# Rebuilding the start-up of a two-layer transformer kernel: first norm transposed on TensorE, bf16 input kept, a second home for one chunk's queries and keys, projections of the third chunk pulled forward

## The chip, the cores and the metric

The kernel runs on one core of one Trainium2 chip. The metric is device time in microseconds, the median of several executions. The kernel before takes 970.37 us (968.58 to 971.06). Ratios are the mean time of one kernel's runs over that of the other's runs of the same rounds, so they are not quite the ratio of the medians quoted beside them. The kernel before was run again in every set of rounds, and its own median lay between 969.2 and 972.0 us; so a difference between medians of different sets is good to some 3 us only, and the ratios decide.

"Chunk" means 512 of the 2048 rows; two layers of four chunks make eight. Attention is done in groups of four heads, eight groups per chunk, six exponentials per group, in three pairs. "Last exponential" means the start of the last of a chunk's 24 pairs, read from the single instructions (the timelines below merge neighbours into one line); the last one ends 1.1 us later. "Block start" means the first matmul of the first feed-forward block: up to there lies the ramp, which is what the change rebuilds.

## The reference

```python
def _A_ref(x, wqkv, wo):            # 32 heads of 18, causal window of 256
    q, k, v = ...                   # x @ wqkv
    scores = einsum("bhqd,bhkd->bhqk", q, k) * (Dh ** -0.5)
    scores = where(mask, scores, -1e9)          # 0 <= i - j < 256
    o = einsum("bhqk,bhkd->bhqd", softmax(scores), v)
    return o.transpose(...).reshape(B, S, D) @ wo

def _B_ref(x, w1, b1, w2, b2):      # D = 576, F = 4608
    h = gelu(_layernorm(x) @ w1 + b1)
    return h @ w2 + b2

x = x + _A_ref(_layernorm(x), ...)  # S = 2048
x = x + _B_ref(_layernorm(x), ...)
x = x + _A_ref(_layernorm(x), ...)  # the same weights again
x = x + _B_ref(_layernorm(x), ...)
```

## The kernel before

Every operation is recorded as a task with an assumed cost. A list scheduler then fixes the order of each engine's instructions; on the chip each engine works through its list in order. Where the scheduler sees a gap on TensorE in the first 140 us, it inserts warm-up matmuls on zeros.

```python
FILL = (6, 5, 4)      # PSUM banks of projections and output matmuls
SC = (0, 2, 4)        # pairs of banks of scores
# schedule(): of all released tasks take the one that can start first
for e in ENGS:
    for t in released[e]:
        st = max(free[e], t.ready)
        ...                                       # and its PSUM banks are free
        key = (round(st, 3), t.prio, t.idx)
        if best is None or key < best[0]:
            best = (key, t, st, got)
_, t, st, got = best
if t.eng == "pe" and st < self.warm_until and st - free["pe"] > 0.4:
    self.keep_warm(free["pe"], st, bank_free, extra)
free[t.eng] = st + t.cost
```

The priority counts only between tasks that can start at the same moment.

```python
def ln_norm_T(t, i, dst, dname, prio, src=None, ...):   # normalise, then transpose
    add("dve", lambda e: e.tensor_scalar(xn[:, sl, 0:D], s[:, t, :], ...), cost=0.6)
    add("sp", lambda e: e.dma_start_transpose(dst[...], xn[:, sl, :]), lat=2.5)

def two_out(lhs, rhs, reads, prio, after=()):  # one projection or output: 2 x 5 matmuls
    bs = [Bank(FILL), Bank(FILL)]
    ...
# tail(k), per tile: output matmuls, residual, norm, and
            add("pool", lambda e, t=t: e.tensor_tensor(x_res[:, t, :], x_res[:, t, :], b2bc[:, :], ALU.add),
                reads=["b2"], writes=X(t), cost=1.4, prio=prio + 3)
# start: the two bias loads first on GpSimd's queue; chunk 0's x, then float32 x of chunk 1
    x_load(CH[1][1], CH[1][2], [f"xa{n0 - 1}"], -6)
```

The softmax here doesn't subtract the row's maximum and nothing guards it: scores larger than these inputs give would overflow.

Of the kernel before, what the change touches and what calls it, by code (L numbers as in the profile page):

```python
# [336 lines left out]
def build_kernel(nc, A_x, A_wqkv, A_wo, B_x, B_w1, B_b1, B_w2, B_b2, out):  # L337
# [56 lines left out]
    fence = sb("fence", [P, 1], FP32)  # L394
# [28 lines left out]

    def dma(q, out_, in_, reads=(), writes=(), cls="w", ring=8, **kw):
        n = 2 if cls != "xr" else 4
        for s in out_.shape:
            n *= s
        add(q, lambda e: e.dma_start(out_, in_), reads=reads, writes=writes, dma=cls, ring=ring, lat=1.3, move=n / 270e3, **kw)

    n0 = CH[0][2]  # L430
    dma("sp", x_in[:, 0:n0, :], x_dram[0:n0 * P, :].rearrange("(t p) d -> p t d", p=P), writes=[f"xin{t}" for t in range(n0)], cls="x",
        ring=4, cost=0.6, prio=-10)
# [7 lines left out]
    def x_load(a, cnt, reads, prio):  # L440

        dma("pool", x_res[:, a:a + cnt, :], x_dram[a * P:(a + cnt) * P, :].rearrange("(t p) d -> p t d", p=P), reads=reads,
            writes=[r for t in range(a, a + cnt) for r in X(t)], cls="xr", ring=8, cost=1.2, prio=prio)
# [3 lines left out]
    add("pool", lambda e: e.memset(nhalf[:, :], -0.5), writes=["nhalf"], cost=0.1, prio=-10)  # L447
    add("pool", lambda e: e.memset(xn[:, :, D:KD * 128], 0.0), writes=[f"xn{i}" for i in range(NXN)], cost=0.4, prio=-10)
    add("pool", lambda e: e.memset(vA[:, :, :, DH:VW], 1.0), writes=[f"v{s}h{h}" for s in range(VS) for h in range(2)], cost=1.6, prio=-8)
    for i in range(NQN):  # L450
# [5 lines left out]
    dma("pool", b2bc[:, :], bass.AP(tensor=B_b2.tensor, offset=B_b2.offset, ap=[[0, P], [1, D]]), writes=["b2"], cls="b", ring=2,  # L456
        cost=1.0, prio=-7)

    def load_b1(e):
        src = bass.AP(tensor=B_b1.tensor, offset=B_b1.offset, ap=[[1, P], [P, NF], [1, 1]])  # L460
        with nc.allow_non_contiguous_dma(reason="bias column layout (init only)"):
            return e.dma_start(b1col[:, :], src)
    add("pool", load_b1, writes=["b1"], dma="b", ring=2, cost=2.0, lat=10.0, prio=-7)

# [12 lines left out]
    def ln_stats(t, prio, src=None, srcres=None):  # L477
        for i in range(2):
            res = [f"x{t}h{i}"] if srcres is None else [srcres]
            s = x_res if src is None else src  # L480
            add("dve", lambda e, i=i, s=s: e.bn_stats(st_all[:, t, i, :], s[:, t, i * HB:(i + 1) * HB]),  # L481
                reads=res, writes=[f"st{t}_{i}"], cost=0.43, prio=prio)
        add("dve", lambda e: e.bn_aggr(mv_all[:, t, :], st_all[:, t, :, :]), reads=[f"st{t}_0", f"st{t}_1"], writes=[f"mv{t}"],  # L483
            cost=0.21, prio=prio)
# [14 lines left out]
    def ln_norm_T(t, i, dst, dname, prio, src=None, srcres=None, dup=False):  # L499
        s = x_res if src is None else src  # L500
        res = X(t) if srcres is None else [srcres]
        sl = xn_ctr[0] % NXN
        xn_ctr[0] += 1
        add("dve", lambda e: e.tensor_scalar(xn[:, sl, 0:D], s[:, t, :], mv_all[:, t, 0:1], rstd[:, t:t + 1],  # L504
                                              op0=ALU.subtract, op1=ALU.mult),
            reads=res + [f"mv{t}", f"rstd{t}"], writes=[f"xn{sl}"], cost=0.6, prio=prio)
        rd = [f"xn{sl}"]
        if dup:
            add("dve", lambda e: e.tensor_scalar(xn[:, sl, D:KD * 128], s[:, t, 512:D], mv_all[:, t, 0:1], rstd[:, t:t + 1],  # L509
                                                  op0=ALU.subtract, op1=ALU.mult),  # L510
                reads=res + [f"mv{t}", f"rstd{t}"], writes=[f"xd{sl}"], cost=0.12, prio=prio)
            rd.append(f"xd{sl}")
        add("sp", lambda e: e.dma_start_transpose(dst[:, :, i * 128:(i + 1) * 128], xn[:, sl, :]),
            reads=rd, writes=[f"{dname}{i}"], dma="t", ring=8, cost=1.3, lat=2.5, move=0.6, prio=prio)
# [26 lines left out]
    def two_out(lhs, rhs, reads, prio, after=()):  # L541

        bs = [Bank(FILL), Bank(FILL)]
# [13 lines left out]
    def qkv(k, i, prio):  # L557
        l, t0, nt = CH[k]
        A = l * NT + t0 + i
        for n, w in enumerate("qkv"):  # L560
            dest = [f"v{A % VS}h{o}" for o in range(2)] if w == "v" else [f"qn{qn_ctr[0] % NQN}h{o}" for o in range(2)]
            bs = two_out(lambda c: xnTa[:, c, i * 128:(i + 1) * 128], lambda c, s, n=n: wqkv[:, c, n * D + s:n * D + s + HB],
                         [f"w{w}A", f"w{w}B", f"w{w}C", f"xa{i}"], prio + 0.01 * n, after=dest)
# [6 lines left out]
            else:  # L570
# [7 lines left out]
                if w == "q":  # L578
                    dst, dn = qT[:, :, i * 128:(i + 1) * 128], f"q{i}"
                else:  # L580
                    dst, dn = kT[:, :, A % KS, :], f"k{A % KS}"
# [16 lines left out]
    def scores(k, g, parts, prio):  # L598
        l, t0, nt = CH[k]
        T0 = l * NT + t0  # L600
        sl = pcount[0] % PS
# [3 lines left out]
        def fn(e):  # L605
            ins = None
            for (so, qo, nq, col) in parts:
                for j in range(4):
                    ins = e.matmul(two(bs[j // 2])[:, j % 2, col:col + nq * 128], kT[32 * j:32 * j + 32, g, (T0 + so) % KS, :],  # L609
                                   qT[32 * j:32 * j + 32, g, qo * 128:(qo + nq) * 128], start=True, stop=True, tile_position=(32 * j, 0))  # L610
            return ins
        rd = [f"q{qo + i}" for (so, qo, nq, col) in parts for i in range(nq)] + [f"k{(T0 + p[0]) % KS}" for p in parts]
# [31 lines left out]
    def pv(k, g, parts, sl, first, last, prio):  # L644
# [18 lines left out]
        if last:  # L663
# [3 lines left out]
                prio=prio)  # L667
# [4 lines left out]
                prio=prio)  # L672
# [23 lines left out]
    def tail(k, prio):  # L696
# [5 lines left out]
        for i in range(nt):  # L702
# [3 lines left out]
            for o in range(2):  # L706
# [4 lines left out]
            add("pool", lambda e, t=t: e.tensor_tensor(x_res[:, t, :], x_res[:, t, :], b2bc[:, :], ALU.add),  # L711
                reads=["b2"], writes=X(t), cost=1.4, prio=prio + 3)


    def G_part(k, hf, prio):
# [6 lines left out]
        while f < f1:  # L722
# [18 lines left out]
            for ff, bk in zip(fs, bks):  # L741
                fl = ff - hf * NFH

                def fn(e, ff=ff, sl=sl, bk=bk):
# [8 lines left out]
                    reads=[bk, "b1"], writes=[f"h{fl}"], cost=0.2 + n * 0.00087, lat=0.2, fifo="act", prio=prio)  # L753
            if fs[-1] % 4 == 3:
                w1_load(prio - 2)
        table("exp", prio)
# [43 lines left out]
    for t in range(n0):  # L800
        ln_stats(t, -6, x_in, f"xin{t}")
    for i in range(n0):
        ln_rstd([i], False, -20)
        ln_norm_T(i, i, xnTa, "xa", -6, x_in, f"xin{i}")
    x_load(CH[1][1], CH[1][2], [f"xa{n0 - 1}"], -6)
    w_load(2, ["xa0"])
    for i in range(n0):
        qkv(0, i, -5)
    x_load(0, n0, [f"k{n0 - 1}"], -4)
    def stats0(k):  # L810
# [4 lines left out]
    stats0(1)  # L815
    ln1(1, -0.9)
    add("pool", lambda e: e.memset(fence[:, :], 0.0), reads=[f"xin{t}" for t in range(n0)], writes=[f"h{f}" for f in range(NFH)],
        cost=0.1, prio=-4)
# [5 lines left out]
    for k in range(NK + 1):  # L824
        b = 4 * k
        last = k == NK
        if not last:
            if 0 < k < NK - 1:
                ln1(k + 1, b + 1)
            E(k, range(0, 4), b - 0.5)  # L830
            if k == 0:
                wo_load()
                kk = later[0]
                x_load(CH[kk][1], CH[kk][2], ["aq1"], 0)
                stats0(kk)
# [6 lines left out]
        if k == 1:  # L842
            w2_load(0, 1, True)
            for n, kk in enumerate(later[1:]):
                x_load(CH[kk][1], CH[kk][2], [f"h{6 + 6 * n}"], b + 2)
                stats0(kk)
        if not last:
            E(k, range(4, 8), b + 1.5)
            if k == 0:
                w1_load(-1, ["aq5"])  # L850
                w1_load(-1, ["aq7"])
        if k >= 1:
            mm2(k - 1, 0, b + 2)
            w2_load(1, b + 3)
        if not last:
            if k + 1 < NK:
                for i in range(CH[k + 1][2]):
                    qkv(k + 1, i, b + 2.2 + 0.2 * i)
            tail(k, b + 1.9)
# [56 lines left out]
```

## Time and profile before

| reading | view | value |
|---|---|---|
| TensorE busy | busy table | 933.4 of 967.4 us |
| warm-up matmuls | groups by line | 284, 38.7 us |
| first projection | TensorE timeline | 14.29 us |
| first score exponential | ScalarE timeline | 32.5 us |
| last exponential of chunk 0 | ScalarE's instructions | 78.8 us |
| block start | TensorE timeline | 121.42 us |

The page's busy table, and its rows of TensorE busy and granted TensorE clock in tenths over 40 equal slices of 24.2 us:

```profile
PE 933.4 (96%) x9596; PEld 582.3 (60%) x9596; DVE 324.6 (34%) x803; ACT 588.0 (61%) x705; POOL 370.5 (38%) x507
PE   8898898999999999999999999999999999999998
PEclk9999898999999999999999999999999999999999
```

TensorE is full from the eighth slice on; the loss is in the first seven. But "busy" includes warm-up matmuls. Groups by line (busy us, mean ns of one, idle before):

```profile
L470 PE MATMUL ps<-warm 128*128 128x256 bf16 x284 | 38.7, 289 | 1.1 <-DVE warm L465 1.1
```

The timeline of TensorE (start, length, engine, line, operation, count, and in brackets the idle time before with what ended it):

```profile
1.12 11.92 PE L470 MATMUL ps<-warm 128*128 128x256 bf16 x90 [1.12 <-DVE warm L465]
14.29 6.29 PE L548 MATMUL ps<-wqkv,xnTa 128*128 128x288 bf16 x50 [1.26 <-DMA xnTa<-xn]
...
32.15 0.34 PE L609 MATMUL ps<-qT,kT 32*128 32x384 bf16 x4
...
121.42 0.61 PE L736 MATMUL ps<-xnTm,w_sb 64*128 64x512 bf16 x4
```

Nothing but filler runs for 14.29 us: tile 0's statistics start when the input is there, at 5.95; the reciprocal root stands behind the issue of a bias load on GpSimd (7.58 to 9.48); and the norm, done at 10.57, goes through a DMA transpose, the last 3.7 us. ScalarE's timeline in chunk 0's attention shows two speeds:

```profile
54.23 1.94 ACT L618 ACTIVATE pT<-ps 128x1024 bf16<-128x1024 f32 x2 [0.96 <-PE ps L609]
57.31 0.60 ACT L618 ACTIVATE pT<-ps 128x512 bf16<-128x512 f32 x1 [1.14 <-PE ps L609]
...
59.30 1.51 ACT L618 ACTIVATE pT<-ps 128x768 bf16<-128x768 f32 x2 [0.91 <-PE ps L609]
...
67.62 4.39 ACT L618 ACTIVATE pT<-ps 128x1024 bf16<-128x1024 f32 x6 [0.84 <-PE ps L609]
72.31 4.39 ACT L618 ACTIVATE pT<-ps 128x1024 bf16<-128x1024 f32 x6 [0.31 <-PE ps L609]
77.00 2.92 ACT L618 ACTIVATE pT<-ps 128x1024 bf16<-128x1024 f32 x4 [0.30 <-PE ps L609]
```

From 67.62 to 72.31 a group takes 4.69 us, nearly all ScalarE's own 4.39. From 44 to 59 us, with chunk 1's projections running, the exponentials wait about 1 us each time for scores, and a group takes about 7.5 us. Later, VectorE's norms and GpSimd's bias adds stand in each other's way. VectorE's timeline, then GpSimd's:

```profile
98.84 1.34 DVE L504 TENSOR_SCALAR xn<-x_res,mv_all,rstd 128x576 bf16<-128x576 f32 x1 [0.55 <-POOL rstd L494]
...
101.49 1.65 DVE L504 TENSOR_SCALAR xn<-x_res,mv_all,rstd 128x576 bf16<-128x576 f32 x1
...
103.65 0.56 DVE L504 TENSOR_SCALAR xn<-x_res,mv_all,rstd 128x576 bf16<-128x576 f32 x1
```

```profile
101.42 1.40 POOL L711 TENSOR_TENSOR x_res<-x_res,b2bc 128x576 f32<-128x576 f32 x1
```

The norm at 103.65 us takes 0.56 us; beside GpSimd's add it takes 1.65 (the one of 1.34 us lies beside a mask of GpSimd, 98.77 to 99.87). The Trainium skill, "SBUF — State Buffer", section "SBUF: two separate sides", says that these two engines contend, for some kinds of instruction, for one shared port pair, locked for a whole instruction, so that the other blocks. The times fit: the two long norms ended 0.32 and 0.31 us after GpSimd's instruction.

### The profile page before, as it was taken

The numbers are of one execution on the slowest core, as the hardware profiler recorded it, in microseconds if no ns is written. First come the engines' busy times: TensorE is split into PE (matmuls) and PEld (weight loads), VectorE is DVE, ScalarE is ACT, GpSimd is POOL, SyncE is SP. The second block draws the span as 40 slices with busy tenths as digits, with TensorE's granted clock in tenths as the row PEclk, the third lists the DMA queues.
The fourth block names the chain that finished last, engine by engine and source line by source line (L and its number), as shares of the span: only waits on it lengthen the run. The fifth ranks groups of instructions, "written<-read, shape, count | busy, mean of one in ns | idle before, by whom it ended". The sixth has DMA issues, their size and how long they took to land.

```text
span 967.4 us, 23096 instructions
## 1 busy us (share of the span) xinstructions
PE 933.4 (96%) x9596; PEld 582.3 (60%) x9596; DVE 324.6 (34%) x803; ACT 588.0 (61%) x705; POOL 370.5 (38%) x507
## 2 busy tenths in 40 slices
PE   8898898999999999999999999999999999999998
PEld 6665545656575655746476564756556464656556
DVE  5653711533037331454038240362214410133001
ACT  0466666478763768557761777737675487862531
POOL 4465815345153443335153251534333351532000
PEclk9999898999999999999999999999999999999999
DMA  9957380993359442694619633495527916084540
GB/s 194 178 122 137 78 250 9 209 194 112 98 127 177 102 138 72 133 204 94 182 58 197 149 112 98 78 224 114 155 68 150 201 45 196 21 219 124 179 135 25
DMA packets 242264, 129.59 MB, mean 134 GB/s; under 512 B 161393, under 2 KB 239985, under 8 KB 242161
## 3 DMA queue, kind: packets, MB, share of 16 engines
q1 hardware_dynamic: 232848, 120.43, 53.0%
q0 software_dynamic: 6880, 5.03, 2.7%
q10 hardware_dynamic: 2432, 2.65, 0.9%
q8 instruction: 76, 1.25, 0.5%
q14 instruction: 28, 0.22, 0.1%
HBM read 90.69 MB, written 2.36 MB: 96 GB/s over the span
## 4 chain that ended last, share of the span: by engine, by line
PE 82%; DMA 6%; POOL 4%; DVE 3%; issue 2%; ACT 2%; SPq 0%; POOLq 0%; DVEq 0%
PE ps L772 29%; PE ps L748 24%; PE ps L548 12%; PE ps L656 7%; PE ps L609 6%; PE ps L736 4%; POOL pT L639 2%; ACT pT L618 2%; DMA attT<-attq 2%; DVE x_res L690 1%; DMA xnTa<-xn 1%; DVE st_all L481 1%; DMA x_res<-in_A_x_dram 1%; DMA kT<-qn 1%; DMA xnTm<-xn 1%
## 5 line engine op out<-in xcount | busy, mean ns | idle before, releaser
L618 ACT ACTIVATE pT<-ps 128x1024 bf16<-128x1024 f32 (+2 forms) x384 | 347.8, 970 | 140.8 <-PE ps L609 139.1
L639 POOL TENSOR_SCALAR_AFFINE_SELECT pT<-pT 128x512 bf16<-128x512 bf16 (+1 forms) x368 | 279.2, 782 | 355.2 <-ACT pT L618 339.0
L751 ACT ACTIVATE hT<-ps,b1col 128x512 bf16<-128x512 f32 x288 | 197.9, 688 | 215.7 <-PE ps L748 215.1
L772 PE MATMUL ps<-w_sb,hT 128*128 128x288 bf16 x2304 | 316.8, 288 | 5.6 <-DVE x_res L690 3.6
L748 PE MATMUL ps<-xnTm,w_sb 128*128 128x512 bf16 x1152 | 266.3, 380 | 0.0
L772 PEld LDWEIGHTS ps<-w_sb,hT 128*128 128x128 bf16 x2304 | 211.3, 98 | 81.6 <-issue 19.6
L748 PEld LDWEIGHTS ps<-xnTm,w_sb 128*128 128x128 bf16 x1152 | 105.8, 98 | 141.1 <-issue 28.6
L690 DVE TENSOR_TENSOR x_res<-ps,x_res 128x288 f32<-128x288 f32 x160 | 71.0, 449 | 352.5 <-PE ps L772 323.3
L548 PE MATMUL ps<-wqkv,xnTa 128*128 128x288 bf16 x960 | 129.9, 287 | 5.1 <-DMA xnTa<-xn 2.1
L656 PEld LDWEIGHTS ps<-vA,pT 128*128 128x128 bf16 x2880 | 95.4, 96 | 26.9 <-issue 8.0
L548 PEld LDWEIGHTS ps<-wqkv,xnTa 128*128 128x128 bf16 x960 | 89.1, 98 | 34.4 <-issue 4.7
L656 PE MATMUL ps<-vA,pT 128*128 128x20 bf16 x2880 | 100.4, 172 | 7.0 <-POOL pT L639 3.8
L609 PE MATMUL ps<-qT,kT 32*128 32x384 bf16 (+2 forms) x1408 | 74.5, 279 | 6.6 <-ACT pT L618 4.3
L575 DVE CAST qn<-ps 128x288 bf16<-128x288 f32 x128 | 58.2, 456 | 39.3 <-PE ps L548 38.6
L504 DVE TENSOR_SCALAR xn<-x_res,mv_all,rstd 128x576 bf16<-128x576 f32 x60 | 44.8, 754 | 43.2 <-DMA xnTm<-xn 26.2
L481 DVE BATCH_NORM_STATS2 st_all<-x_res 128x6 f32<-128x288 f32 x120 | 51.0, 445 | 18.9 <-DMA x_res<-in_A_x_dram 17.5
L711 POOL TENSOR_TENSOR x_res<-x_res,b2bc 128x576 f32<-128x576 f32 x32 | 45.7, 1429 | 26.9 <-DVE xn L509 23.6
L492 POOL TENSOR_SCALAR vtmp<-mv_all 128x1 f32<-128x1 f32 (+1 forms) x43 | 8.5, 198 | 103.2 <-DVE mv_all L483 100.5
L609 PEld LDWEIGHTS ps<-qT,kT 32*128 32x128 bf16 x1408 | 22.4, 92 | 42.5 <-issue 25.2
L548 PE MATMUL ps<-wo_sb,attT 128*128 128x288 bf16 x320 | 43.2, 286 | 4.3 <-DMA attT<-attq 3.1
L693 DVE TENSOR_TENSOR xn<-ps,x_res 128x288 bf16<-128x288 f32 x32 | 14.7, 458 | 93.3 <-PE ps L772 93.3
L736 PE MATMUL ps<-xnTm,w_sb 64*128 64x512 bf16 x288 | 45.0, 382 | 0.9 <-ACT pT L618 0.9
(30 smaller groups left out, 290.0 us busy)
## 6 DMA issues: line engine op xcount, KB each, us to landing
w_sb<-in_B_w_dram SPq DMA_DIRECT2D x144, 288.0 KB, 5.0
w_sb<-in_B_w_dram SPq DMA_DIRECT2D x72, 512.0 KB, 4.2
w_sb<-in_B_w_dram SPq DMA_DIRECT2D x144, 32.0 KB, 3.8
x_res<-in_A_x_dram POOLq DMA_DIRECT2D x4, 1152.0 KB, 7.0
out_dram<-xn SPq DMA_DIRECT2D x16, 144.0 KB, 2.0
wqkv<-in_A_wqkv_dram ACTq DMA_DIRECT2D x3, 576.0 KB, 6.0
hT<-in_A_x_dram SPq DMA_DIRECT2D x1, 576.0 KB, 5.1
wo_sb<-in_A_wo_dram ACTq DMA_DIRECT2D x1, 576.0 KB, 3.9
```

The source lines that it names most:

```text
L481: add("dve", lambda e, i=i, s=s: e.bn_stats(st_all[:, t, i, :], s[:, t, i * HB:(i + 1) * HB]), reads=res, writes=[f"st{t}_{i}"], cost=0.43 ...
L548: ins = e.matmul(bank(bs[o])[:, 0:HB], lhs(c), rhs(c, o * HB), start=(c == 0), stop=(c == KD - 1))
L575: add("dve", lambda e, o=o, b=bs[o], qv=qv: e.tensor_copy(qv[:, o * 16:(o + 1) * 16, 0:DH], bank(b)[:, 0:HB].rearrange("p (h d) -> p h d", ...
L609: ins = e.matmul(two(bs[j // 2])[:, j % 2, col:col + nq * 128], kT[32 * j:32 * j + 32, g, (T0 + so) % KS, :], qT[32 * j:32 * j + 32, g, qo ...
L618: add("act", lambda e, h2=h2: e.activation(pT[:, sl, 2 * h2:2 * h2 + 2, lo:hi], two(bs[h2])[:, :, lo:hi], ACT.Exp, scale=SCALE), reads=[bs ...
L639: add("pool", lambda e, ap=ap, pat=pat, sgn=sgn, kind=kind: e.affine_select(ap, ap, pattern=pat, compare_op=(ALU.is_ge if kind == "d" else ...
L656: ins = e.matmul(bank(B_O)[:, o:o + VW], pT[:, sl, j, col + qi * 128:col + (qi + 1) * 128], vA[:, (T0 + so) % VS, 4 * g + j, :], start=(fi ...
L690: add("dve", lambda e: e.tensor_tensor(x_res[:, t, sl], bank(b)[:, 0:HB], x_res[:, t, sl], ALU.add), reads=[b], writes=[f"x{t}h{hh}"], cos ...
L736: ins = e.matmul(bank(bk)[:, 0:n], w1_sb[64 * b:64 * b + 64, sl, col:col + 128], xnTm[64 * b:64 * b + 64, k % 2, 4, 0:n], start=True, stop ...
L748: ins = e.matmul(bank(bk)[:, 0:n], w1_sb[:, sl, col:col + 128], xnTm[:, k % 2, c, 0:n], start=False, stop=(c == 3))
L751: add("act", lambda e, ff=ff, fl=fl, bk=bk: e.activation(hT[:, fl, 0:n], bank(bk)[:, 0:n], ACT.Gelu_apprx_tanh, bias=b1col[:, ff:ff + 1]), ...
L772: ins = e.matmul(bank(b)[:, 0:HB], hT[:, fl, i * 128:(i + 1) * 128], w2_sb[:, fl, hh * HB:(hh + 1) * HB], start=(fl == 0), stop=(fl == NFH ...
```

## The change

The intent is to fill the some 50 us of the ramp (38.7 of filler, 15.0 idle) in which TensorE has nothing useful to do: an earlier first projection, an earlier first score, and chunk 2's projections (120 matmuls, 60 of which the kernel before does after the block start) as useful filler in the ramp. The core of the diff:

```diff
+    qx = x_res[:, 12:16, :]...bitcast(BF16)...      # second home of chunk 1's queries
+    kx = x_res[:, 8:12, :]...bitcast(BF16)...       # and keys, in rows not loaded yet
+    def q_of(k):
+        return (qx, "qx") if k == 1 else (qT, "q")
...
+    for a, cnt in ((0, 1), (1, 1), (2, 2)):         # tile 0 arrives first
+        xin_load(a, cnt)
-    dma("pool", b2bc[:, :], ...)                     # bias loads, first on the queue
-    add("pool", load_b1, ..., prio=-7)
+    add("pool", load_b1, reads=["xa3"], ..., prio=-1)
...
+        if pe:                                       # in ln_norm_T, first four tiles
+            b = Bank(FILL)
+                for c in range(KD):
+                    ins = e.transpose(bank(b)..., xn[:, sl, c * 128:(c + 1) * 128], ident[:, :])
+            add("act", lambda e: e.copy(dst[...], bank(b)...), cost=0.75)
+            return
...
+    QK0 = {("q", 0): -5.0, ("k", 0): -4.9, ...}      # queries and keys before values
-             [...], prio + 0.01 * n, after=dest)
+             [...], prio + 0.01 * n, after=dest, fill=(6,) if k == 1 else FILL)
...
-            add("pool", ... b2bc ..., reads=["b2"])           # tail(): moved
+            if hf == 0 and fs[0] // 4 < nt:                    # into the feed-forward part
+                add("pool", ... b2bc ..., reads=["b2", f"h{fs[0]}"])
...
-    x_load(CH[1][1], CH[1][2], [f"xa{n0 - 1}"], -6)
+    xin_load(4, 4, ["xa0"], -6)                      # bf16 input of chunks 1 and 2 kept in
+    xin_load(8, 4, ["k3"], -4)                       # the space of the feed-forward result
+    ln1_in(1, -0.9)                                  # norms straight from the bf16 input
...
+            if k == 0:
+                ln1_in(2, 1)                         # chunk 2's norms in the ramp
```

## The prediction

> **What bounds the kernel.** TensorE is busy 933 of 967 us (busy table); the chain of waits is 82% TensorE. From 160 us on it is busy 98% or more of nearly every 20 us window at granted clock 1.00, so every later stage is useful TensorE work that the change leaves alone. What can be saved is in the ramp. There TensorE's "busy" is partly filler: the group of warm-up matmuls has 284 instructions at about 0.113 us apart (8 took 0.9 us), 32 us. With some 15 us idle that is about 48 us without useful work before the first feed-forward block starts at 121.4 us (timeline).
>
> Where those 48 us are (timeline, chain): 14.3 us until the first projection (input 5.1 us, reciprocal root delayed by the 1.9 us bias load on GpSimd, DMA transpose 3.6 us); first scores only at 32.2 us, because the last key transposes took 7.9 us beside the 1.15 MB float32 load of x; chunk 0's attention, with chunk 1's projections in the same PSUM banks, takes 32.5 to 82 us, though alone it runs at 4.7 us a group (ScalarE 4.39), 37.5 us for eight; from 62 us TensorE has nothing but filler, since chunk 2 cannot be projected; then chunk 1's queries wait for transposes (83 to 88), and 98 to 104 us stand still while VectorE's float32 norm (1.3 to 1.65 us against 0.58 alone) and GpSimd's bias adds (1.4 us) alternate. The Trainium skill, "SBUF - State Buffer", says those two engines share a port pair held for a whole instruction; the trace agrees.
>
> **What the change does.** 20 TensorE transposes (the skill's "TensorE: Matmul & The Clock Gate", Part 4, gives 275 to 390 ns in isolation; no trace here shows one; I estimate 0.6 us for five pipelined) and four ScalarE copies (about 0.8 us) replace four DMA transposes; tile 0 arrives first; the bias loads come later. First projection: about 8.8 us. Scores start at 22 to 26 us: 16 evictions at 0.61 us plus statistics on VectorE, and eight transpose issues at 1.4 to 1.9 us. Chunk 0's attention then runs near ScalarE's rate, end 62 to 66 us; half of chunk 1 (6.1 us a group, four groups) ends near 91. TensorE's useful work up to there is 400 projection matmuls (49.4 us at 0.1235), 40 output ones (4.9), attention 27, in all 82 us from 8.8: again 91. Both limits are tight, so I add 5 us for their friction: first feed-forward block at 96 us (91 to 103) instead of 121.4, with all of chunk 2 projected instead of half (60 matmuls, 7.4 us). Expected gain 33 us.
>
> Given back: the second half of chunk 1's attention loses those 60 matmuls of filler and becomes ScalarE-bound at its end (3 to 5 us idle, maybe a cold clock; before, 140 to 160 us also ran at 0.83). Chunks 2 and 3's x loads come later, which should stay hidden. Net about 30 us: **940 us, 8 in 10 between 927 and 954**; faster by over 2%: 0.82, within 2%: 0.16, slower: 0.02.
>
> **Right if:** warm-up matmuls fall to 71; first projection at 8 to 10 us; first score exponential at 22 to 26 us; exponentials of chunk 0 with under 15% idle; no 5 us hole near 100 us; first feed-forward block at 91 to 103 us; windows after 200 us unchanged.
>
> **Wrong if:** the one PSUM bank left to chunk 1's projections (matmuls, then eviction, serial) or the now more crowded transposes (x, queries, keys, and the b1 load's small packets at 12 us) slow chunk 0's attention; chunk 1 waits for its queries; or the saved time returns as idle TensorE in chunk 1's second half because projections there are gone.

## The result and the profile after

The changed kernel takes **957.20 us** (955.22 to 957.70), ratio 0.9863 with a 95% interval of 0.9847 to 0.9879. It is 13.2 us faster, which is within 2%, and slower than the whole predicted range of 927 to 954. All outputs are right.

| | before | predicted | after |
|---|---|---|---|
| warm-up matmuls | 284 | 71 | 71 |
| first projection, us | 14.29 | 8.8 | 9.23 |
| first exponential | 32.5 | 22–26 | 25.8 |
| end of chunk 0's attention (end of its last exponential) | 79.9 | 62–66 | 77.2 |
| block start | 121.42 | 96 (91–103) | 110.27 |
| block start to end | 846.0 | +3 | 843.6 |
| projections before the block | 300 | all of chunk 2's | 360 |

The page after, busy table, slices and warm-up group:

```profile
PE 914.3 (96%) x9403; PEld 564.0 (59%) x9403; DVE 313.7 (33%) x804; ACT 590.7 (62%) x709; POOL 369.1 (39%) x507
PE   8799899999999999999999999999999999999998
PEclk9799999999999999999999999999999999999999
```

```profile
L490 PE MATMUL ps<-warm 128*128 128x256 bf16 x71 | 12.3, 335 | 1.1 <-DVE warm L485 1.1
```

Filler fell from 38.7 to 12.3 us. But the second slice has a clock of 0.7: the ramp now has a cold spot there, where the kernel before had none (its own, of 0.8, is in the fifth slice). TensorE's timeline after:

```profile
7.92 0.44 PE L539 MATMUL ps<-ident,xn 128*128 128x128 bf16 x5
...
9.23 1.39 PE L580 MATMUL ps<-wqkv,xnTa 128*128 128x288 bf16 x10 [0.22 <-ACT xnTa L542]
...
25.40 0.34 PE L646 MATMUL ps<-qT,kT 32*128 32x384 bf16 x4 [2.78 <-DMA qT<-qn]
...
33.86 0.79 PE L580 MATMUL ps<-wqkv,xnTa 128*128 128x288 bf16 x5 [0.23 <-DVE qn L610]
...
36.93 0.29 PE L646 MATMUL ps<-qT,kT 32*128 32x256 bf16 x4 [1.13 <-ACT pT L655]
...
38.33 0.34 PE L646 MATMUL ps<-qT,kT 32*128 32x384 bf16 x4 [0.72 <-ACT pT L655]
...
41.13 1.38 PE L580 MATMUL ps<-wqkv,xnTa 128*128 128x288 bf16 x5
...
110.27 0.61 PE L771 MATMUL ps<-xnTm,w_sb 64*128 64x512 bf16 x4
```

ScalarE's timeline after: the first two exponentials, the next six, and the last two of chunk 0:

```profile
25.79 1.51 ACT L655 ACTIVATE pT<-ps 128x768 bf16<-128x768 f32 x2 [12.24 <-PE ps L646]
30.68 4.51 ACT L655 ACTIVATE pT<-ps 128x1024 bf16<-128x1024 f32 x6 [3.38 <-PE ps L646]
...
76.08 1.08 ACT L655 ACTIVATE pT<-ps 128x512 bf16<-128x512 f32 x2 [0.53 <-PE ps L646]
```

The start went as predicted. Then, from 34 to 40 us, TensorE has holes of 0.7 to 1.1 us, and at 41.13 a projection of five matmuls takes 1.38 us instead of 0.79: the clock has dropped. Windows of 10 us (busy time with count of TensorE, weight load, VectorE, ScalarE and GpSimd, then granted clock, DMA share, GB/s):

```profile
30.00:40.00 10.00, 7.08 (x118) 4.46 (x119) 6.19 (x19) 8.65 (x12) 5.66 (x8) 0.99 0.73 118
40.00:50.00 10.00, 9.03 (x115) 5.29 (x112) 4.88 (x12) 6.45 (x9) 6.91 (x11) 0.67 0.74 168
```

VectorE's timeline in those holes shows what holds the projections up:

```profile
34.16 1.18 DVE L501 BATCH_NORM_STATS2 st_all<-hT 128x6 f32<-128x288 bf16 x3 [0.36 <-DMA hT<-in_A_x_dram]
...
36.17 0.81 DVE L501 BATCH_NORM_STATS2 st_all<-hT 128x6 f32<-128x288 bf16 x2
...
37.01 0.77 DVE L501 BATCH_NORM_STATS2 st_all<-hT 128x6 f32<-128x288 bf16 x2
...
37.80 0.41 DVE L501 BATCH_NORM_STATS2 st_all<-hT 128x6 f32<-128x288 bf16 x1
38.12 0.44 DVE L610 CAST qn<-ps 128x288 bf16<-128x288 f32 x1
```

The projection that started at 33.86 us was done by 34.7 (33.86 + 0.79). Its eviction, the CAST, started at 38.12, behind eight statistics instructions of chunk 2, though the first of chunk 2's projections runs only at 69.0 us (the 241st projection matmul). Chunk 1's projections have one PSUM bank, so no other could start until then.

Where the time went can be added up. At the full clock a projection matmul took 0.1235 us. Work up to the block start is 360 × 0.1235 = 44.5 us of projections, 4.9 of output matmuls, about 26.2 of scores and attention products, and 1.3 of transposes: 77 us. The other 33 us of the 110.3 are some 15.5 of idle time, 11.8 of filler and about 6 of projections slowed by the cold clock or by waiting. Of these 33 us, about 9 lie before the first projection, 5.5 from there to 30 us, 7 to 8 from 30 to 50, 3 to 4 in the rest of chunk 0's attention, and 9 in chunk 1's half.

After the block start, TensorE has 60 projections (7.4 us) less to do, but that part is only 2.4 us shorter: 5.0 us were given back. Most of it shows in one group, the output projections after 125 us, in the kernel before and then in the changed kernel:

```profile
L548 PE MATMUL ps<-wo_sb,attT 128*128 128x288 bf16 x280 | 37.8, 286 | 3.9 <-DMA attT<-attq 2.8 <-DVE x_res L690 1.0
```

```profile
L580 PE MATMUL ps<-wo_sb,attT 128*128 128x288 bf16 x280 | 37.5, 286 | 7.7 <-DMA attT<-attq 6.5 <-DVE x_res L727 1.2
```

Their idle time grew from 3.9 to 7.7 us, 3.8 of the 5.0; nearly all of that is the wait for the transposed attention (2.8 and 6.5).

### The profile page after: what moved, and what is told of

The parts are those of the page before. It is cut to its first block, busy times and chain, and to the rows that moved or that the text cites. A ratio compares the mean times of both kernels' runs of the same rounds, so it can differ in the third digit from the quotient of the medians. Undisturbed runs are those within 1.5% of the kernel's fastest.

```text
span 953.9 us, 22759 instructions
## 1 busy us (share of the span) xinstructions
PE 914.3 (96%) x9403; PEld 564.0 (59%) x9403; DVE 313.7 (33%) x804; ACT 590.7 (62%) x709; POOL 369.1 (39%) x507
## 5 line engine op out<-in xcount | busy, mean ns | idle before, releaser
L580 PE MATMUL ps<-wqkv,xnTa 128*128 128x288 bf16 x960 | 135.0, 290 | 4.7 <-DVE qn L610 2.0
L580 PEld LDWEIGHTS ps<-wqkv,xnTa 128*128 128x128 bf16 x960 | 88.8, 99 | 37.5 <-DVE qn L610 5.4
L693 PEld LDWEIGHTS ps<-vA,pT 128*128 128x128 bf16 x2880 | 95.0, 96 | 26.2 <-issue 9.4
L646 PE MATMUL ps<-qT,kT 32*128 32x384 bf16 (+2 forms) x1216 | 64.6, 278 | 8.5 <-ACT pT L655 4.8
L501 DVE BATCH_NORM_STATS2 st_all<-x_res 128x6 f32<-128x288 f32 x104 | 44.8, 447 | 13.8 <-DMA x_res<-in_A_x_dram 12.7
L646 PEld LDWEIGHTS ps<-qT,kT 32*128 32x128 bf16 x1216 | 19.6, 92 | 39.6 <-issue 23.2
L524 DVE TENSOR_SCALAR xn<-x_res,mv_all,rstd 128x576 bf16<-128x576 f32 x52 | 31.6, 610 | 34.0 <-DMA xnTm<-xn 23.0
```

The costliest lines, as they stand in the source:

```text
L580: ins = e.matmul(bank(bs[o])[:, 0:HB], lhs(c), rhs(c, o * HB), start=(c == 0), stop=(c == KD - 1))
L646: ins = e.matmul(two(bs[j // 2])[:, j % 2, col:col + nq * 128], k_of(T0 + so)[0][32 * j:32 * j + 32, g, :], qs[32 * j:32 * j + 32, g, qo * ...
L693: ins = e.matmul(bank(B_O)[:, o:o + VW], pT[:, sl, j, col + qi * 128:col + (qi + 1) * 128], vA[:, (T0 + so) % VS, 4 * g + j, :], start=(fi ...
```

## The experiments

Besides these two, eighteen kernels ran on the chip. Unless said otherwise an edit is against the changed kernel. The table collects the readings; columns 3 to 6 come from each kernel's one profiled run. "Rest" is the time from the block start to the end, less 0.1235 us for each projection that is left over to it (360 less column 5), so that kernels which moved work across the block start can be compared. "Late order" says whether TensorE's last 6000 instructions (fillers left out) stand as in the changed kernel (A), as in w2 (B), or nearly so; it was read from the built programs, and its meaning comes out only with the last experiments.

| run | median us (ratio) | last exp. of chunk 0 | block start | projections before it | rest | late order |
|---|---|---|---|---|---|---|
| before | 970.37 | 78.8 | 121.42 | 300 | 838.6 | own |
| after | 957.20 (0.9863) | 76.1 | 110.27 | 360 | 843.6 | A |
| u1_banks | 958.63 (0.9895) | 78.8 | 107.95 | 360 | 846.9 | B |
| u2_nohome | 971.64 (1.0019) | 81.5 | 119.44 | 340 | 847.8 | near A |
| u3_dmat | 961.67 (0.9922) | 82.2 | 117.43 | 360 | 843.3 | A |
| u4_noch2 | 961.82 (0.9902) | 70.4 | 99.37 | 240 | 845.9 | A |
| v1_nohome_clean | 964.83 (0.9953) | 76.6 | 115.57 | 340 | 846.0 | near A |
| v2_biaslate | 959.56 (0.9889) | 77.5 | 114.47 | 360 | 843.8 | A |
| v3_fillholes | 956.92 (0.9871) | 77.6 | 112.21 | 360 | 840.0 | A |
| v4_truelat | 966.16 (0.9963) | 81.6 | 115.66 | 360 | 848.1 | near B |
| w1_alone | 981.91 (1.0123) | 67.2 | 134.53 | 360 | 845.6 | A |
| w2_evictfirst | 957.77 (0.9872) | 71.3 | 104.73 | 360 | 853.5 | B |
| w3_scoresfirst | **947.56 (0.9784)** | 68.4 | 101.19 | 325 | 839.6 | A |
| w4_cut | 949.12 (0.9786) | 68.5 | 99.02 | 325 | 843.8 | A |
| x1_ruleonly | 958.96 (0.9864) | 72.2 | 113.50 | 360 | 844.6 | A |
| x2_rule76 | 954.75 (0.9821) | 68.6 | 104.29 | 355 | 849.2 | B |
| x3_beforerule | 963.93 (0.9928) | 74.5 | 111.50 | 265 | 838.1 | own |
| y1_hold | 956.81 (0.9862) | 72.7 | 104.31 | 330 | 846.5 | B |
| y2_holdonly | 960.96 (0.9897) | 77.3 | 109.39 | 330 | 846.3 | B |
| z1_lateorder | **950.83 (0.9805)** | 72.4 | 105.78 | 360 | 842.6 | A |

Theory at the outset: chunk 0's attention is slow because something in the changed ramp stretches it. Rivals were the one PSUM bank, crowded transposes, and projections standing before scores in TensorE's list.

### One bank or three

```diff
-  prio + 0.01 * n, after=dest, fill=(6,) if k == 1 else FILL)
+  prio + 0.01 * n, after=dest, fill=FILL)
```

> One part undone: chunk 1's projections may again use PSUM banks 6, 5 and 4 instead of bank 6 alone. Theory 'one bank': in the changed kernel a projection of chunk 1 and its eviction follow each other serially (1.34 us a piece where five matmuls take 0.62), so giving the banks back starts the first feed-forward block 3 us or more before the changed kernel's 110.3 us and the time falls to about 953. Rival 'shared banks were the trouble' (the prediction's view): chunk 0's attention returns towards 7.5 us a group as in the kernel before, the first feed-forward block comes 3 us or more later, time about 960 or more. If neither matters: within 1.5 us of 957.2.

Chunk 0's attention did not get shorter: 47.8 us from its third exponential (31.0) to its last (78.8), against 45.4 in the changed kernel. The block started 2.3 us earlier, the total did not fall. So the one bank is not what keeps the attention from ScalarE's rate. The Trainium skill, "Perfetto Trace Analysis", section "Matmul Optimizations", advises using all eight banks. Both kernels do; what u1 adds is that chunk 1's projections may take three of them, and then 206 instead of 165 projection matmuls ran between the third and the last exponential. The 2.3 us fell away behind the block (rest 846.9 instead of 843.6), which was understood only at the end.

### What each part is worth, by undoing it

Second home off (u2), and again with the float32 loads of chunks 2 and 3 held back, which only the second home's bookkeeping had delayed (v1):

```diff
-    Q1 = 4
+    Q1 = -99
-        return (qx, "qx") if k == 1 else (qT, "q")
+        return (qT, "q")
-        sl = A if A < Q1 else (A - 2) % KS
+        sl = A % KS
-                    x_load(CH[kk][1], CH[kk][2], [], b + 2)        # v1 only
+                    x_load(CH[kk][1], CH[kk][2], ["aq7"], b + 2)   # v1 only
```

> One part undone: queries and keys of chunk 1 go to the shared query and key tiles again, all else as in the changed kernel. Theory 'the second home carries the gain': the first scores of chunk 1 wait again for transposes after chunk 0's last group, 5 us or more of filler and idle TensorE come back between the two chunks' attention, and the time rises to 961 to 966. Rival 'projections are available anyway': less than 1.5 us change from 957.2.

> The run without a second home once more, cleanly: in the earlier one the loads of x for chunks 2 and 3, which had waited for the second home to be read, went out at the start and crowded the transposes (first exponential 32.8 us). Here these loads wait for the end of chunk 1's attention as they do in the changed kernel, and the first 80 us of TensorE's order are the changed kernel's. Theory 'second home carries the gain': first exponential back at 26 us, but a stretch of projections without exponentials between chunk 0's and chunk 1's attention, time 961 to 966. Rival 'the crowding alone cost the 14 us': within 2 us of 957.2.

u2 was no clean experiment: the big loads went out at once, and the transposes of queries then took 9.4 us to land instead of 5.5. v1 is the clean one: 964.83 us, so the second home is worth 7.6 us (8.7 by the ratios).

DMA transposes for the first norm again (`pe=True` removed from the call), and chunk 2 out of the ramp (its statistics gated on the end of chunk 0):

```diff
-        ln_norm_T(i, i, xnTa, "xa", -6, x_in, [f"xin{i}"], pe=True)   # u3
+        ln_norm_T(i, i, xnTa, "xa", -6, x_in, [f"xin{i}"])            # u3
-            if k == 0:                                                # u4
-                ln1_in(2, 1)                                          # u4, and after tail():
+                ln1_in(2, 1, ['xm0_3'])                               # u4
```

> One part undone: the first norm is transposed by DMA again, all else as in the changed kernel. If the start is on the critical path one for one: first projection 2 to 4 us later than 9.2 us, first score exponential as much later than 25.8, and the time up by the same 2 to 4 us (about 960). Rival 'the start is hidden behind the transposes of queries and keys': first projection later, first score exponential within 1 us of 25.8, time within 1 us of 957.2.

> One part undone: chunk 2's norm waits for chunk 0's feed-forward input, so none of its projections run in the ramp. Theory 'filler grain' (each projection of 0.62 us put between scores delays the exponentials, and TensorE, not ScalarE, paces chunk 0's attention): the first feed-forward block starts at 95 to 101 us instead of 110.3, chunk 1's first half runs at 6.1 to 6.5 us a group, but the 120 projection matmuls (14.8 us) come back later as work, so the total is 955 to 962. Rival 'ScalarE paced already': the first block moves by less than 4 us and the total rises by 8 us or more, to 965 to 970.

The TensorE transposes are worth 4.5 us, chunk 2 in the ramp 4.6 us (5.7 and 3.8 by the ratios). The three parts sum to 16.7, more than the 13.2 of the whole change; they overlap, and each run has its own static order: in u3 the first projection comes 1.9 us later, but the block start 7.2. u4 is telling in another way: without chunk 2 the last exponential of chunk 0 is at 70.4, and chunk 1's half runs from 71.57 to 99.63:

```profile
68.55 12.29 ACT L655 ACTIVATE pT<-ps 128x1024 bf16<-128x1024 f32 x14 [0.32 <-PE ps L646]
...
97.69 1.94 ACT L655 ACTIVATE pT<-ps 128x1024 bf16<-128x1024 f32 x2 [0.84 <-PE ps L646]
```

That is 28.1 us, against 33.5 in the changed kernel (77.52 to 111.04) and 24.4 in the prediction. So chunk 2's work accounts for some 5 of the 9 us over; the rest is there without it.

### Crowded transposes, a cold hole, and the scheduler's assumed latency

The two bias issues moved to about 60 us in GpSimd's list, nothing else (v2); 42 fillers put into the holes from 22 to 30 us (v3); the scheduler told the latency that the trace shows for chunk 0's transposes (v4):

```diff
-        order = sorted(order + extra, key=lambda x: x[0])
+        order = sorted([(62.0 if t.dma == "b" else st, t) for st, t in order] + extra, ...)   # v2
+        order = sorted(order + extra + self.holes(order), key=lambda x: x[0])                 # v3
-   dma="t", ring=8, cost=1.3, lat=2.5, ...
+   dma="t", ring=8, cost=1.3 if k else 1.9, lat=2.5 if k else 4.0, ...                        # v4
```

> The static order of the changed kernel, with only the two bias loads moved later in GpSimd's stream (to about 60 us), away from the query and key transposes. Theory 'crowded transposes': the 4-byte-packet load (10.3 us to landing, beside query transposes of 5.5 us) delays the first scores; without it the query transposes land in 3 to 4 us, first exponential at 22 to 24 us instead of 25.8, third at 26 to 28 instead of 30.7, first feed-forward block 2 to 4 us earlier, time 953 to 955. Rival 'the order, not the arrival, sets the pace': exponentials start earlier but the first feed-forward block stays within 1.5 us of 110.3 and the time within 1.5 us of 957.2.

> The static order of the changed kernel, with 42 filler matmuls put into the waits between 22 and 30 us. Theory 'cold clock': the granted clock, 0.83 at 20 to 30 us and 0.67 at 40 to 50 us in the changed kernel, is lost because TensorE stands still there, and returns to 0.95 or more; TensorE wins 3 to 4 us before 50 us, and the time falls to 953 to 955. Rival 'the clock is low where TensorE has slack anyway': clock up, first feed-forward block and time within 1.5 us.

> Only the scheduler's assumption about chunk 0's query and key transposes is changed, nearer to what the trace shows (1.9 us of issue and 4.0 to landing instead of 1.3 and 2.5), so the static order of all engines is made anew. Theory 'the order was made for transposes that land too early': the value projections fill the hole at 22.6 to 25.4 us, idle before the first feed-forward block falls by 3 us or more from 15.3, the time falls by 2 to 4 us. Rival 'the waits only move': within 2 us of 957.2.

v2: the bias loads (288 KB, and 18 KB in 4-byte packets; which of the two matters was not separated) do crowd the transposes. With both moved away, the queries' transposes land in 4.1 instead of 5.5 us, and the first exponential comes 2.4 us earlier. By 51 us the lead was gone in a wait of 1.84 us for a norm's transpose, and the block started later than in the changed kernel. v3: the window from 20 to 30 us kept its full clock (1.00 instead of 0.83), but 40 to 50 us fell to 0.56 all the same; no gain. v4: 9 us slower, although the scheduler was told figures nearer to the trace; every order here is fixed in advance, and a small change of an assumption re-deals it. So crowding is real and not the bound, and the first hole is not the costly one.

### Projections and scores

All of chunk 1's projections held back until chunk 0's attention is done (w1; it also had to mend a latent race that this order exposed), and chunk 2's statistics given a lower priority, so that evictions go first (w2):

```diff
-   [..., f"xa{i}"], prio + 0.01 * n, ...                               # w1
+   [..., f"xa{i}"] + (["aq7"] if k == 1 else []), prio + 0.01 * n, ...  # w1
-                ln1_in(2, 1)                                            # w2
+                ln1_in(2, 2.95)                                         # w2
```

> The projections of chunk 1 (and so those of chunk 2) wait until chunk 0's attention is done; all else is the changed kernel. Slower on purpose. Theory 'projections between the scores stretch chunk 0's attention': the first-to-48th exponential of chunk 0 takes 37 to 41 us instead of 50.3 (third to 48th: 34 to 37 instead of 45.4), with ScalarE over 90% busy, though the transposes are as crowded and the start is the same. Rival 'late transposes, masks on GpSimd or the cold clock pace it': the third-to-48th distance stays above 42 us. Total 975 to 990 us either way.

> One number changed: chunk 2's norm on VectorE has lower priority than the evictions of chunk 1's projections. In the changed kernel an eviction of the single bank stood 3.6 us behind chunk 2's statistics (TensorE done at 34.5, eviction at 38.1). Theory 'the single bank is blocked by the norm': exponentials of chunk 0 close up by 2 us or more (third to 48th under 43.5 us instead of 45.4), first feed-forward block at 106 to 108 us, total 954 to 956. Rival 'TensorE's sharing alone sets the pace': within 1.5 us of 110.3 and 957.2.

w1 confirms that projections stretch the attention: third to last exponential in 37.1 us instead of 45.4, though the kernel as a whole is slower, since the projections come later. It also shows that ScalarE's rate is not reached even so: after a first group of 7.0 us, the groups take 4.6 to 5.9, and the last exponential ends at 68.3, past the predicted 62 to 66. ScalarE's timeline of w1, where a group takes 4.69 us (34.74 to 39.43):

```profile
34.74 4.45 ACT L655 ACTIVATE pT<-ps 128x1024 bf16<-128x1024 f32 x6 [0.19 <-PE ps L646]
39.43 2.92 ACT L655 ACTIVATE pT<-ps 128x1024 bf16<-128x1024 f32 x4 [0.24 <-PE ps L646]
```

w2 keeps the projections and gets 41.3 us. Its block starts at 104.73 us, 5.5 us earlier than in the changed kernel with the same 360 projections done. (The same edit separates y1 from y2 below, where it is worth 5.1 us: 104.31 and 109.39.) The eviction that stood until 38.12 in the changed kernel now has a place of its own between the statistics, on VectorE's timeline of w2; below it the block start:

```profile
34.00 0.46 DVE L610 CAST qn<-ps 128x288 bf16<-128x288 f32 x1
```

```profile
104.73 0.61 PE L771 MATMUL ps<-xnTm,w_sb 64*128 64x512 bf16 x4 [0.25 <-ACT pT L655]
```

The windows of w2 to set against those of the changed kernel above:

```profile
30.00:40.00 10.00, 8.73 (x138) 5.42 (x137) 6.64 (x19) 9.04 (x13) 6.17 (x9) 1.00 0.92 152
40.00:50.00 10.00, 8.60 (x126) 5.31 (x123) 6.43 (x16) 7.71 (x11) 8.48 (x13) 1.00 0.91 186
```

TensorE is busy 8.73 instead of 7.08 us of the first window, and the clock of the second is 1.00 instead of 0.67. Over the whole ramp, the clock lost to throttling (10 us times one minus the granted clock, summed over the windows) is 1.7 us in w2 and 6.8 in the changed kernel. That the difference, 5.1, explains the 5.5 is not shown: between y2 and y1 the clock lost differs by 8.5 us (10.2 and 1.7), the block start by 5.1. The same pairing is in the other runs: in all eight kernels made from the changed one, itself included, with under 7.8 us of busy TensorE from 30 to 40 us (after, u1, u2, v1, v2, v3, x1, y2), the clock from 40 to 50 was 0.53 to 0.83. In eight of the ten with more it was 1.00; the other two, u3 and v4, dropped to 0.66 in a second window that was itself only 6.8 and 6.0 us busy. The Trainium skill, "TensorE: Matmul & The Clock Gate", Part 1, tells of a gate with two states, set by how busy a free-running window of about 3.4 us was. The clock records of the trace, which the windows of 10 us average, agree: the changed kernel ran at half clock from 39.81 to 46.64 us, twice 3.41 us, and in the 3.41 us before that TensorE was busy for 1.97 us, 58%; in w2, which stayed at full clock, it was busy for 3.18 us of the same stretch.

Yet w2's total stayed at 957.77 us. The 5.5 us disappeared behind the block.

### Two attempts to keep it

A rule in the scheduler (w3, on top of w2; w4 also moves one group of chunk 1's attention behind the block): in the ramp a projection is not started if more urgent TensorE work becomes ready within 0.6 of its time.

```diff
             _, t, st, got = best
+            if YS > 0 and t.eng == "pe" and st < YEND and t.prio > YP:  # 0.6, 125 us, -0.3
+                for u in released["pe"]:
+                    if u is t or u.prio > t.prio - 0.3:
+                        continue
+                    su = max(free["pe"], u.ready)      # and its banks
+                    if su < st + YS * t.cost and (alt is None or su < alt[0]):
+                        alt = (su, u, gu)
+                if alt is not None:
+                    st, t, got = alt
-                ln1_in(2, 1)
+                ln1_in(2, 2.95)
+    CUT = {0: 4, 1: 3}                                                  # w4 only, else {0: 4, 1: 4}
```

> As the run before it, and in the ramp the scheduler does not start a projection if a score becomes ready before 60% of the projection has passed. Theory 'projections between the scores stretch the attention': third to 48th exponential of chunk 0 40 to 43 us, first feed-forward block 102 to 106 us; but as TensorE's sum of work is the same and it idles more, at most half of what the block moves shows in the total: 952 to 955. Rival 'the order is not what matters': within 1.5 us of the run before it.

> As the run before it, and three instead of four groups of chunk 1's attention before the first feed-forward block. Theory 'the sum of TensorE's work decides, not where the block starts': the block starts 4 us or more earlier than in the run before it, yet the total moves by less than 2 us. Rival 'an earlier block is an earlier end': the total falls by 4 us or more.

w3 beats both kernels: 947.56 us, 9.6 less than the changed kernel (7.7 by the ratios, whose intervals do not touch). w4's block starts 2.2 us earlier still, with one group of attention less before it, and its ratio is the same (0.9786 and 0.9784): an earlier block start alone is not an earlier end. It was tempting to say that the order of projections against scores had been the cause. The next runs took that apart:

- x1_ruleonly: the rule with `ln1_in(2, 1)` as in the change.
- x2_rule76: w3 with the rule ending at 76 instead of 125 us of the scheduler's time.
- x3_beforerule: the same rule in the kernel before.

> The scheduler rule alone (in the ramp a projection is not started where more urgent TensorE work becomes ready within 0.6 of its time), statistics of chunk 2 where the change has them. If the order of projections against scores is the cause, this alone recovers most: last exponential of chunk 0 at 69 to 72 us, mean clock over 0.995, total 947 to 951. Rival, that rule and later statistics are needed together (evictions stuck behind the statistics): last exponential past 74 us, total 954 to 958.

> Rule and later statistics, the rule only in the part that the scheduler models before 76 us (chunk 0's attention). If the gain comes from chunk 0's attention, the total stays at 947 to 951 with the last exponential of chunk 0 at 69 us. If it comes from chunk 1's first half or from the clock there, 953 to 958.

> The same scheduler rule in the kernel before, which has four banks for the projections of chunk 1 and no projections of chunk 2 in the ramp. If the rule only mends what the change worsened, it is worth under 4 us here (967 to 972). If projections ahead of scores cost the kernel before as much, it is worth 7 to 11 us (959 to 963), and the change's own worth is unaltered.

x1 gains nothing in the total (958.96), which neither expectation had quite: chunk 0's last exponential comes at 72.2 instead of 76.1, but chunk 1's half takes 40.9 us instead of 33.5. The clock from 40 to 50 us is 0.53, and an eviction still stands behind the statistics (projection done by 37.1, eviction at 38.96). x2 ends chunk 0's attention within 0.3 us of w3; its median is 7.2 us above w3's, but by the ratios it is 3.6 us and the intervals overlap, so that x2 is slower is not clear. And x3 gains 7.0 us by the ratio (8.0 by the medians of its own rounds) in the kernel before, where nothing of the change is present: third to last exponential in 38.1 us instead of 42.4, with the same banks (three for the projections, not the four of the expectation) and about as many projection matmuls in between (107 instead of 112). The end of chunk 0's attention in x3:

```profile
36.36 4.39 ACT L637 ACTIVATE pT<-ps 128x1024 bf16<-128x1024 f32 x6 [2.45 <-PE ps L628]
...
72.66 2.92 ACT L637 ACTIVATE pT<-ps 128x1024 bf16<-128x1024 f32 x4 [0.24 <-PE ps L628]
```

So the loss from that order was in the kernel before too. It is tempting to add that the change neither made nor removed it, since the ratio of w3 to x3, 0.9784 / 0.9928 = 0.9855, is nearly that of the change itself, 0.9863. But w3 has the later statistics as well; with the rule alone in both kernels (x1 to x3) the change is worth 0.9864 / 0.9928 = 0.9936 only. In the changed kernel the rule pays only together with the later statistics.

Corrected for work moved, w3's ramp is not better than w2's: 101.19 + 35 × 0.1235 = 105.5 against 104.7. All of its lead over w2 is in the rest, 839.6 against 853.5. The next guess was that the 35 projections left over fill TensorE behind the block. y1 leaves 30 there by hand on w2, y2 on the changed kernel:

```diff
-   [..., f"xa{i}"], prio + 0.01 * n, ...
+   [..., f"xa{i}"] + (["h16"] if k == 2 and i == 3 else []), prio + 0.01 * n, ...
```

> Statistics of chunk 2 late as in w2, and nothing else but that the 30 projection matmuls of chunk 2's last tile wait for the first feed-forward block, so 330 instead of 360 come before it, as 325 do in w3. If w3 beats w2 because matmuls are left to fill TensorE behind the block, the total is 947 to 951 here too, without any rule for the order, with the block at 100 to 102 us, waits of the output projections after 125 us under 6 us instead of 11.5 and mean clock over 0.995. Rival, the order within chunk 0's attention is what w3 needs: 956 to 959, and only the block starts earlier by the 3.7 us moved.

> The changed kernel with the same 30 matmuls held back, statistics of chunk 2 where the change has them. If filler behind the block is worth its gain by itself, 950 to 953. If the ramp's loss of 5.5 us (evictions behind the statistics) must go as well, 956 to 959 with the block at 106 to 107 us.

The guess was wrong: 956.81 and 960.96 us, no gain in either.

### The order of the later stages

Comparing the built programs gave the answer's first half. The order of TensorE's last 6000 instructions, long after any edit, is one of two: order A in the changed kernel, w3 and w4, order B in w2, x2, y1, y2 and u1. The scheduler works forward in its own time, so a ramp that ends at another moment can tip all later choices. In the table, the rest is 839.6 to 845.9 us in A and 846.3 to 853.5 in B. The two ranges nearly touch, so the order is not a fixed cost: y1, y2 and u1 are within 3.3 us of the changed kernel, w2 is 9.9 above it. The last run gives w2's ramp the order A, by one pause of 1.0 us in the scheduler's own time after 200 us; no instruction is added:

```diff
             free[t.eng] = st + t.cost
+            if t.eng == "pe" and st > BUMP:                  # BUMP = 200, once
+                free["pe"], BUMP = free["pe"] + 1.0, 1e9
```

> w2's kernel; in the scheduler's model alone, TensorE pauses 1.0 us once after 200 us, no instruction is added. TensorE's first 2166 instructions without filler (to some 200 us) stand as in w2, its last 6339 as in the changed kernel and in w3. If the later order is what ate w2's 5.5 us, the first feed-forward block stays at 104 to 106 us, the rest from there takes 842 to 846 us instead of 853.5, the total is 948 to 952. If not, the total stays at 956 to 959.

It took 950.83 us (950.15 to 952.74), ratio 0.9805 with an interval of 0.9782 to 0.9828 that lies clear of w2's 0.9846 to 0.9898. Block start 105.78 us, rest 842.6. The ramp's gain was real; w2's later order had eaten it. Windows of w2:

```profile
390.00:400.00 10.00, 8.46 (x53) 5.33 (x53) 6.27 (x18) 0.69 (x1) 1.47 (x4) 0.83 0.97 200
620.00:630.00 10.00, 8.24 (x50) 4.95 (x49) 6.36 (x18) 0.69 (x1) 1.47 (x4) 0.83 1.01 149
```

and of z1_lateorder:

```profile
390.00:400.00 10.00, 9.68 (x62) 5.05 (x61) 8.59 (x26) 3.26 (x5) 2.43 (x8) 1.00 0.93 220
620.00:630.00 10.00, 10.00 (x52) 4.17 (x51) 5.85 (x16) 6.51 (x10) 1.81 (x4) 1.00 0.85 181
```

The output projections after 125 us, in w2 and then in z1_lateorder:

```profile
L580 PE MATMUL ps<-wo_sb,attT 128*128 128x288 bf16 x280 | 42.4, 306 | 11.5 <-DMA attT<-attq 9.7 <-DVE mv_all L503 1.4 <-DVE x_res L727 0.4
```

```profile
L583 PE MATMUL ps<-wo_sb,attT 128*128 128x288 bf16 x280 | 37.8, 287 | 6.2 <-DMA attT<-attq 4.1 <-DVE mv_all L506 1.4 <-DVE x_res L730 0.7
```

In w2 they wait 5.3 us longer and take 19 ns more each; the clock, as the windows show, is cold in places. Against the changed kernel, w2's part behind the block has 4.8 us more idle TensorE (24.5 against 19.7) and about 5.1 us more clock lost (6.8 against 1.7): 9.9 together, as much as the difference of the two rests, though clock lost while TensorE waits costs nothing.

## Why the prediction was wrong

**Right:** what bounds the kernel; 71 warm-up matmuls; first projection at 8.8 us (9.23); first exponential at 22 to 26 us (25.8); chunk 2's projections all before the block; no 5 us hole near 100 us any more.

**Wrong, the step that failed:** "Chunk 0's attention then runs near ScalarE's rate, end 62 to 66 us". It ended at 77.2. Exponentials were to idle under 15%; they idled 30% (35.9 us busy of 51.4). The prediction had seen 7.5 against 4.7 us a group in the profile of before, and laid the difference to shared PSUM banks, which the change unshares. u1 shows that the banks are not it. w1 shows that the projections' presence is most of it (third to last 37.1 us without them, end at 68.3), and x3 that their order is, in the kernel before as well (38.1 us with the same banks). The change left that order rule alone, and put chunk 2's statistics before evictions besides: with those later, w2 ends 4.7 us earlier. And 4.7 us was the best stretch: without projections, w1's first group took 7.0 us, so all eight took 42.2 instead of the 37.5 that the prediction reckoned with.

**Wrong in the same way:** half of chunk 1 at 6.1 us a group, 24.4 us. It took 33.5 (77.52 to 111.04, start of the first to end of the last exponential of that half). u4 has 28.1 without chunk 2's projections, so they are only part of it; the other 3.7 us were not traced. The prediction took the larger of two limits, ScalarE's and TensorE's, with 5 us for both. Both were tight, and each engine waited for the other in turn.

**The mis-sized term:** 5 us for friction. From the first projection on, 24 us were not useful work (33 − 9). The sum hid part of the error, because the 400 projections in it are 360: the 40 output matmuls are in both of its terms, 4.9 us too much. It also put the filler of before at 32 us, where the group shows 38.7. Of the friction 5.5 us are shown to be one thing: evictions behind chunk 2's statistics in VectorE's list, with what followed from it, a cold clock among it (w2; 5.1 us between y2 and y1). The prediction did not look at what VectorE's order would be, though the built program lists it.

**Given back:** 5.0 us instead of 3, mostly in waits of the output projections for transposed attention. The prediction expected idle time only in chunk 1's second half, and "windows after 200 us unchanged"; but a changed ramp re-dealt the order of the later stages, which the prediction had not considered.

**"Wrong if"** named the one bank (2.3 us earlier with three banks, in a single profile), crowded transposes (true: 5.5 to 4.1 us to landing, but worth nothing in time) and saved time coming back later (true).

**Still open:** why order B waits longer at chunk boundaries was not followed instruction by instruction. Not all of the remaining friction was found: the best ramp here with all the work in it, w2's, still starts its block at 104.7 us instead of the predicted 96. And why w3 has a rest 3 us better than z1's with the same late order is not settled; part may be the phase of the clock gate, which no run shows; what they show is that w3's six runs spread from 946.45 to 954.23 us with mean clocks from 0.998 down to 0.993.

## What to carry to other kernels

In a kernel whose order is fixed in advance, an added early task costs most where it lands in front of another engine's small, urgent task: list the order of every engine, and ask of each inserted instruction what waits behind it. When two limits are both nearly full, do not take the larger one; look for a stretch of the profile in which both kinds of work ran together, and use its rate. And before calling a ramp gain lost or an idea worthless, compare the later stages instruction by instruction: here a different late order hid a real gain of 5 us, and only a run with the late order restored could tell.

## What the Trainium skill lacked or had wrong

- "TensorE: Matmul & The Clock Gate", Part 4: it gives about 390 ns for one 128×128 bf16 transpose in isolation and about 275 ns in one kernel's context. Five in a row took 0.44 us here in all, about 65 ns each in the sum over the ramp (20 in 1.3 us). The page has no figure for transposes in a pipelined row.
- The same page, Part 1 and "HAM oscillation": its abstract rule is to have no idle gaps over about 3.4 us. In the changed kernel the clock was at half from 39.81 to 46.64 us although no gap from 26 to 50 us was longer than 1.13 us; TensorE was busy 58% of the 3.41 us before. Its second failure mode, micro-idling between groups, is nearer to this, but has no number for it. Counted over the twenty profiles, after the first 10 us and in the steps of 3.41 us in which the clock changed: of the windows at full clock, 70 were followed by half clock, none of them busier than 74%, and no window under 42% kept the full clock; in between both happened.
- "DMA: Bandwidth & Descriptors": the page has no number for what a load of small packets does to transposes that are in flight beside it. A load of 18 KB in 4-byte packets took 10.3 us to land, and moving it away together with a load of 288 KB brought the queries' transposes from 5.5 to 4.1 us and the keys' from 4.8 to 3.7.
- "Perfetto Trace Analysis", "Matmul Optimizations": the advice to use all eight banks does not say how to share them out. Three banks instead of one for chunk 1's projections gained nothing here (0.9895 and 0.9863, with intervals that overlap). Nor does that section speak of the order in which independent work is put on one engine, which moved the total by 7 us without any other change (w2 to z1_lateorder).
